# Narrowing float64 weights: a parametric ReLU on ScalarE carries the sign, in place of a VectorE instruction

## The chip, the cores and the metric

The kernel runs on one core of one Trainium2 chip. The metric is the device time of one execution in microseconds (us). Of the kernel before, three runs were timed, and one more execution was taken with the hardware profiler. All timelines below are of that profiled execution, with 0 at the start of its span.

## What is computed

Three blocks follow each other, on 2 batches of 768 positions and a width of 512:

```
# attention: 8 heads of 64; a window of +-15 positions, and 24 block summaries
k_sum = k.reshape(B, H, nb, block, D).max(axis=3)
v_sum = v.reshape(B, H, nb, block, D).mean(axis=3)
a = softmax([scale * q @ k.T in the window, scale * q @ k_sum.T + log(block)])
x = a @ [v, v_sum]
# gated block: 512 -> 1024, a convolution of 3 taps over the positions, 1024 -> 512
h = np.maximum(x @ w_in, 0.0)
conv_out = sum(conv_w[k] * hp[:, k:k + S, :] for k in range(3))
x = h * sigmoid(conv_out) @ w_out
# second block: layer norm, 512 -> 2048 -> 512, and a residual
xn = (x - mu) / np.sqrt(var + 1e-06) * g_ln
out = x + np.maximum(xn @ w_ch1, 0.0) @ w_ch2
```

The activations are float32. The five weights `w_in`, `conv_w`, `w_out`, `w_ch1` and `w_ch2` come as float64, and the kernel turns them into float32 itself.

## The kernel before

**Precision.** Each product of the two dense blocks is made of three matmuls in fp32r: an operand is split into a high part (the value rounded to fp32r) and a low part (what is left), and high*high, high*low and low*high are summed in PSUM. So every weight tile needs a high and a low half before its products can run, and every activation tile too.

**Narrowing.** A float64 weight lies in SBUF as two 32-bit words, the more significant one at the odd place. `weight_ops` (L687) makes of a tile of 128x512 weights its two fp32r halves in six steps, each an operation of its own in the plan:

- z, `narrow_0` (L664), VectorE: the lower word is shifted right by 29, which leaves the three mantissa bits that a float32 still needs from it.
- a, `narrow_1` (L668), VectorE: the sign bit of the upper word is put into bit 31 of the lower word (an AND and an OR in one instruction).
- b, `narrow_2` (L674), ScalarE: the upper word, read as a float32, is multiplied by 2^-112 and its absolute value is taken. Read this way, eight of the eleven exponent bits stand where float32 has its exponent; the factor takes off the difference of the two biases, and the sign goes.
- c, `narrow_3` (L678), VectorE: the upper word is shifted left by three, and the lower word is ORed in: the float32.
- d, ScalarE (L692): the high half. It is followed by e, GpSimd (L694): the low half by a subtraction.

There are 48 such tiles: 8 of `w_in` (names wst and x2a in the profile), 8 of `w_out` (wst), and 32 of the second block (raw; 16 pairs, one of `w_ch1` and one of `w_ch2` for each of 16 slices m of the 2048 columns). The 24x128 tile of `conv_w` (craw) takes the same way in `c1` to `c3` (L894 to L900).

**The work.** Attention goes by 24 windows of 64 positions, four to a group (L497 to L614): scores (sc, L502), their maximum (X, L521), exponentials (prob, L533), the sum's reciprocal (L541, L545), a product (N, L552), a transposition (P, L562), the product with v (av, L582) and its split into the high and low half of xT (L611 gives the low one). The gated block goes by 48 steps i, eight to a group of four windows: three products h (L753), ReLU (L765), three taps on VectorE (c, L781), tanh (L786), gate (g, L794), its split (ghi L805, glo L812), and eight steps later two output tiles x (L825). Step 24 is the first of group 3, the first of the second batch; it needs the low halves of windows 12 to 16. For the second block each batch needs a layer norm: statistics (L1061), normalization (xn, L1120), 32 block transpositions (xf, L1132) and a split (xnT, L1141 gives the low half). Then, in the order of `order` (L1083), for each pair of a batch and a slice m come two halves of ch (L1201, evacuated by L1208 and L1212, two PSUM banks in turn) and six accumulating tiles acc (L1236). The first eight slices of batch 0 come first, then batch 1 with all 16, then the last eight of batch 0.

**What sets the order.** No engine's order is written by hand. Each of these pieces of work is an operation of `Plan` (L26) with an engine, a guessed cost, the operations that it comes after, rings of buffers that it takes and gives back, and a due time. `arrange` (L77) lays them out in one pass: of those that could start soonest it takes the one with the earliest due time, moved by a table of numbers for each kind (`BIAS`, in `KNOBS`, L3). Due times run backwards through the dependencies and subtract the costs (L71 to L75). The kernel then emits all operations by the planned start. So an operation that is taken out also changes the due times and the places of others, on all engines. The numbers of `KNOBS` choose the engine of each operation by its kind and number, so no work goes to another engine.

Each engine runs its instructions in the order given. Loads are issued by SyncE's queue. The raw tiles of the second block have two buffers; the load for slice m waits until e of slice m-2 is done.

Of the kernel before, what the change touches and what calls it, by code (L numbers as in the profile page):

```python
# [13 lines left out]
U32 = mybir.dt.uint32  # L14
BF16 = mybir.dt.bfloat16
AF = mybir.ActivationFunctionType
ALU = mybir.AluOpType
# [2 lines left out]

NEG = -1e9
F64_SCALE = 2.0 ** -112
LN32 = (3.46875, -0.003021240234375, 7.152557373046875e-06)


# [169 lines left out]
def local_summary_attention_moe_kernel(  # L195
# [34 lines left out]
    V, A, G, T = nc.vector, nc.scalar, nc.gpsimd, nc.tensor  # L230
    if O('CAL', '0') == '1':
        import builtins
        V, A, G, T = (builtins.PROXY(x, y) for x, y in ((V, 'V'), (A, 'A'), (G, 'G'), (T, 'P')))
# [51 lines left out]
    plan = Plan()  # L285
# [58 lines left out]
    def make_mask_r(e):  # L344
# [8 lines left out]
        ln = mask_r[64:67, :, 0:NB]  # L353
        G.memset(ln, LN32[0])
        for i in (0, 1):
            G.affine_select(out=ln, in_=ln, compare_op=ALU.is_ge, fill=LN32[i + 1], base=i,
                            pattern=[[0, 3], [0, NB]], channel_multiplier=-1)
# [306 lines left out]
    def narrow_0(raw):  # L664
        least = raw.bitcast(U32)[..., 0::2]
        V.tensor_scalar(out=least, in0=least, scalar1=29, scalar2=None, op0=ALU.logical_shift_right)  # L666

    def narrow_1(raw):  # L668
        w_ = raw.bitcast(U32)
        most, least = w_[..., 1::2], w_[..., 0::2]  # L670
        V.scalar_tensor_tensor(out=least, in0=most, scalar=0x80000000, in1=least,  # L671
                               op0=ALU.bitwise_and, op1=ALU.bitwise_or)

    def narrow_2(raw):  # L674
        f = raw.bitcast(U32)[..., 1::2].bitcast(F32)
        A.activation(out=f, in_=f, func=AF.Abs, scale=F64_SCALE)  # L676

    def narrow_3(raw):  # L678
        w_ = raw.bitcast(U32)
        most, least = w_[..., 1::2], w_[..., 0::2]  # L680
        V.scalar_tensor_tensor(out=most, in0=most, scalar=3, in1=least,  # L681
                               op0=ALU.logical_shift_left, op1=ALU.bitwise_or)

    def narrowed(raw):
        return raw.bitcast(U32)[..., 1::2].bitcast(F32)

    def weight_ops(name, raw, hi, lo, after, extra=()):  # L687
        a = plan.op(name + "z", (("V", 335),), lambda e: narrow_0(raw()), after)
        a = plan.op(name + "a", (("V", 602),), lambda e: narrow_1(raw()), [a])
        b_ = plan.op(name + "b", (("A", 520),), lambda e: narrow_2(raw()), [a])  # L690
        c_ = plan.op(name + "c", (("V", 602),), lambda e: narrow_3(raw()), [b_])
        d = plan.op(name + "d", (("A", 520),), lambda e: A.copy(hi(), narrowed(raw())), [c_] + list(extra))  # L692
        g = plan.op(name + "e", (("G", 1225),),
                    lambda e: G.tensor_tensor(out=lo(), in0=narrowed(raw()), in1=hi().bitcast(F32), op=ALU.subtract),  # L694
                    [d])
        return [d, g]
# [9 lines left out]
    def weight(j, early_reads):  # L706
        t = w_stage(j)

        def ld():
            if j < NF:  # L710
                nc.sync.dma_start(out=t.bitcast(U32).rearrange("p (c f) -> p c f", c=4),
                                  in_=w_in[:, 256 * j:256 * j + 256].rearrange("(c p) f -> p c f", p=128))
            else:
                nc.sync.dma_start(out=t.bitcast(U32), in_=w_out[128 * (j - NF):128 * (j - NF) + 128, :])
        prev = j - 6 if j in (6, 7, 8) else j - 3 if j > 8 else None
        l = dma(f"lw{j}", 1456, ld, WD[prev] if prev is not None else [])
        if j < NF:
            raw = lambda: t.rearrange("p (c f) -> p c f", c=4)
            hl = [lambda i=i: wi[i][:, :, 128 * j:128 * j + 128] for i in range(2)]
        else:  # L720
            raw = lambda: t

            def piece(i):
                if not wo:
                    wo.extend(m1.tile([128, NF, DM], F32R, tag=f"wo{k_}", name=f"wo{k_}") for k_ in range(2))
                return wo[i][:, j - NF, :]
            hl = [lambda i=i: piece(i) for i in range(2)]
        WD[j] = weight_ops(f"w{'io'[j // NF]}{j}", raw, hl[0], hl[1], [l], early_reads if j >= NF else ())
# [7 lines left out]
    def m_step(i):  # L736
# [81 lines left out]
        for t in range(2):  # L818
# [10 lines left out]
            if f == NF - 1:  # L829
                def fe(e, t=t):  # L830
# [8 lines left out]
    craw = at.tile([24, 256], F32, name="craw")  # L839
    lc = [dma("lc0", 70, lambda: nc.sync.dma_start(out=craw.bitcast(U32),  # L840
                                                   in_=conv_w.rearrange("k (f p) -> (k f) p", p=256))),
# [51 lines left out]

    def c1(e):  # L894
        narrow_0(craw)
        narrow_1(craw)

    def c3(e):
        narrow_3(craw)
# [2 lines left out]
    def c4(e):  # L902
        live["cc"] = bank("x2")
        T.transpose(live["cc"][:, 0:28], crow, ident[0:28, 0:28])

    cc = plan.op("cc1", (("V", 464),), c1, lc[:1])
    cc = plan.op("cc2", (("A", 230),), lambda e: narrow_2(craw), [cc])
    cc = plan.op("cc3", (("V", 464),), c3, [cc])
    cc = plan.op("cc4", (("P", 60),), c4, [cc, ident_op, lc[1]], take=[("x2", "cc")])
# [187 lines left out]
    def w2_ops(m, due):  # L1097
        gate = gate2 if m < NS else gate3
        l = dma(f"lwy{m}", 2912, lambda: w2_load(m), gate2, take=[("raw", m)])
        free = [x for t in range(NT) for x in AC[1, m - 8, t]] if m >= 8 else []  # L1100
        for h in range(2):
            s = slice(h * 512, (h + 1) * 512)
            d, g = weight_ops(f"y{m}{h}", lambda h=h: raws[m][:, h * 1024:(h + 1) * 1024],
                              lambda s=s: slots[m % 8][0][:, s], lambda s=s: slots[m % 8][1][:, s], [l], gate + free)
            g.give.append(("raw", m))
            d.due0 = g.due0 = due
            WD2.setdefault(m, []).extend([d, g])
# [245 lines left out]
```

## Time and profile before

| | |
|---|---|
| runs | 548.56, 549.22, 549.1 us; median 549.1 |
| profiled execution | 548.64 us, of which the span is 546.9 and 1.74 lie outside |
| busy share of the span | PE (TensorE) 92%, DVE (VectorE) 70%, ACT (ScalarE) 43%, POOL (GpSimd) 31% |
| instructions | PE 2830, DVE 711, ACT 623, POOL 192 |
| TensorE's granted clock | 0.991 on average |

In the profile an engine is PE, DVE, ACT, POOL or SP, and PEld is TensorE's weight load. A row of a group reads: line, engine, operation, output<-input, shape, count, then busy time in us and the mean of one in ns, then the engine's idle time ahead of it and what ended that. A chain is followed back from the last instruction: at each step to what released it, or to the instruction ahead of it on its engine. Matmuls overlap, so a busy PE is not a PE at its peak.

### The profile page before, as it was taken

The page shows a single profiled execution, that of the slowest core. Times are in us where ns is not written, and L with a number is a line of the kernel's source. Part 1 is how long each engine was busy: PE and PEld are TensorE (multiplying, and loading weights), DVE is VectorE, ACT ScalarE, POOL GpSimd, SP SyncE. Part 2 cuts the span into 40 slices and gives each one's busy share as a digit, 9 for nine tenths or more (in the row PEclk, how much of TensorE's full clock was granted, in tenths as well). Part 3 has the DMA queues.
Part 4 walks back from the last instruction along what each step waited for, and adds up shares of the span by engine and source line. Part 5 has one row for each costly group of instructions (what it writes and reads, how often), then busy time and mean ns, then how long its engine had stood idle before and what let it go on. Part 6 is the DMA issues. An engine that isn't in the chain of part 4 may idle for free.

```text
span 546.9 us, 7840 instructions
## 1 busy us (share of the span) xinstructions
PE 500.9 (92%) x2830; PEld 438.5 (80%) x2830; DVE 383.5 (70%) x711; ACT 233.9 (43%) x623; POOL 169.4 (31%) x192
## 2 busy tenths in 40 slices
PE   7776788798999999889998879999999999999997
PEld 4565767677989898668787768989889899899895
DVE  5799899999988689999999999417767101221104
ACT  5887577643786555554434243123343101101100
POOL 6349457442722342523335410023423000000000
PEclk9999799899999999999999999999999999999999
DMA  9994364234011004000053440024340000020003
GB/s 279 326 237 113 87 182 132 73 76 95 2 32 43 1 13 155 1 1 2 1 188 120 153 141 14 1 77 119 114 155 1 0 1 0 1 115 1 0 1 115
DMA packets 56034, 43.30 MB, mean 79 GB/s; under 512 B 26080, under 2 KB 50940, under 8 KB 55996
## 3 DMA queue, kind: packets, MB, share of 16 engines
q1 hardware_dynamic: 55852, 42.68, 26.3%
q8 instruction: 22, 0.36, 0.3%
q14 instruction: 16, 0.13, 0.1%
q10 hardware_dynamic: 144, 0.13, 0.1%
HBM read 39.22 MB, written 3.15 MB: 77 GB/s over the span
## 4 chain that ended last, share of the span: by engine, by line
PE 49%; DVE 37%; ACT 6%; issue 4%; POOL 2%; DMA 2%; DVEq 0%; SPq 0%; POOLq 0%; ACTq 0%
PE ch L1201 19%; PE acc L1236 19%; DVE c L781 7%; DVE xf L1132 5%; PE x L825 4%; PE h L753 3%; DVE g L794 3%; DVE xT L611 2%; ACT prob L533 2%; DVE raw L671 2%; DVE wst L671 2%; DMA raw<-in_moe_w_ch_dram 2%; DVE raw L681 2%; PE sc L502 1%; DVE wst L666 1%
## 5 line engine op out<-in xcount | busy, mean ns | idle before, releaser
L1236 PE MATMUL acc<-wh,ch 128*128 128x512 f32 x382 | 124.5, 394 | 0.0
L1212 DVE SCALAR_TENSOR_TENSOR ch<-ch,ch 128x384 fp32r<-128x384 f32 x64 | 34.1, 552 | 120.1 <-ACT ch L1208 119.9
L1201 PE MATMUL ch<-xnT,wh 128*128 128x384 f32 x512 | 101.7, 339 | 8.6 <-DVE ch L1212 7.5
L1201 PEld LDWEIGHTS ch<-xnT,wh 128*128 128x128 f32 x512 | 90.3, 188 | 15.1 <-DVE ch L1212 9.9
L753 PE MATMUL h<-xT,wi 128*128 128x258 f32 x576 | 82.8, 294 | 12.4 <-ACT h L765 11.9
L1208 ACT ACTIVATE ch<-ch 128x384 fp32r<-128x384 f32 x64 | 29.5, 490 | 147.0 <-PE acc L1236 140.4
L753 PEld LDWEIGHTS h<-xT,wi 128*128 128x128 f32 x576 | 75.9, 195 | 19.6 <-ACT h L765 17.2
L1236 PEld LDWEIGHTS acc<-wh,ch 128*128 128x128 f32 x382 | 71.7, 188 | 15.7
L694 POOL TENSOR_TENSOR wl<-raw,wh 128x512 fp32r<-128x512 f32 x32 | 47.0, 1488 | 102.7 <-ACT wh L692 61.1
L1236 PE MATMUL acc<-wl,ch 128*128 128x512 f32 x191 | 75.1, 393 | 0.0
L825 PE MATMUL x<-wo,ghi 128*128 128x512 f32 x192 | 62.2, 403 | 0.7 <-ACT x2b L293 0.6
L812 POOL TENSOR_TENSOR glo<-g,ghi 128x256 fp32r<-128x256 f32 x48 | 41.6, 869 | 65.3 <-ACT ghi L805 64.0
L781 DVE SCALAR_TENSOR_TENSOR c<-h,ccol,c 128x256 f32<-128x256 f32 x96 | 56.6, 603 | 3.4 <-ACT c L293 1.6
L1201 PE MATMUL ch<-xnT,wl 128*128 128x384 f32 x256 | 55.0, 336 | 0.0
L1201 PEld LDWEIGHTS ch<-xnT,wl 128*128 128x128 f32 x256 | 45.3, 188 | 0.1
L1236 PEld LDWEIGHTS acc<-wl,ch 128*128 128x128 f32 x191 | 35.8, 188 | 7.1
L825 PE MATMUL x<-wo,glo 128*128 128x512 f32 x96 | 38.0, 396 | 0.4 <-POOL xT L594 0.4
L825 PEld LDWEIGHTS x<-wo,ghi 128*128 128x128 f32 x192 | 33.3, 189 | 6.2 <-ACT x2b L293 1.1
L533 ACT ACTIVATE prob<-sc,nm 128x120 f32<-128x120 f32 x96 | 33.3, 363 | 10.5 <-DVE nm L521 10.4
L1132 DVE STREAM_TRANSPOSE xf<-xn 32x384 f32<-32x384 f32 x64 | 36.4, 569 | 1.4
L786 ACT ACTIVATE c<-c 128x256 f32<-128x256 f32 x48 | 20.0, 419 | 39.8 <-DVE c L781 39.6
L676 ACT ACTIVATE raw<-raw 128x512 f32<-128x512 f32 x32 | 20.6, 682 | 37.2 <-DVE raw L671 20.9
(140 smaller groups left out, 729.5 us busy)
## 6 DMA issues: line engine op xcount, KB each, us to landing
raw<-in_moe_w_ch_dram SPq DMA_DIRECT2D x32, 512.0 KB, 5.4
wst<-in_moe_w_out_dram SPq DMA_DIRECT2D x8, 512.0 KB, 3.5
vw<-in_v_dram SPq DMA_DIRECT2D x20, 192.0 KB, 3.3
wst<-in_moe_w_in_dram SPq DMA_DIRECT2D x5, 512.0 KB, 5.9
s_q<-in_q_dram SPq DMA_DIRECT2D x4, 512.0 KB, 4.8
early<-in_k_dram SPq DMA_DIRECT2D x3, 512.0 KB
early<-in_v_dram SPq DMA_DIRECT2D x3, 512.0 KB, 6.0
x2a<-in_moe_w_in_dram SPq DMA_DIRECT2D x3, 512.0 KB, 8.4
```

What stands on the lines that cost most here:

```text
L533: A.activation(out=pr[:, p, :], in_=sc[:, p * NK:(p + 1) * NK], func=AF.Exp, bias=nm[:, p:p + 1], scale=1.0, accum_out=sm[:, p:p + 1])
L671: V.scalar_tensor_tensor(out=least, in0=most, scalar=0x80000000, in1=least, op0=ALU.bitwise_and, op1=ALU.bitwise_or)
L694: lambda e: G.tensor_tensor(out=lo(), in0=narrowed(raw()), in1=hi().bitcast(F32), op=ALU.subtract),
L753: T.matmul(live["h", i][:, 0:CH + 2], w_[:, c, f * 128:(f + 1) * 128], x_[:, c, :], start=(k_ == 0 and c == 0), stop=(k_ == 2 and c == 3))
L781: V.scalar_tensor_tensor(out=ct, in0=ht[:, kk:kk + CH], scalar=ccol[:, kk * NF + f:kk * NF + f + 1], in1=ct, op0=ALU.mult, op1=ALU.add)
L812: on[e].tensor_tensor(out=glo, in0=live.pop(("g", i)), in1=live["ghi", i].bitcast(F32), op=ALU.subtract)
L825: T.matmul(x2ps[g, t], l[:, ts_], r[:, f, :], start=(f == 0 and j == 0), stop=(f == NF - 1 and j == 2))
L1132: V.transpose(out=o_, in_=i_)
L1201: T.matmul(cp[:, 0:384], w_[:, c * 128:(c + 1) * 128], x_[:, c, s], start=(n_ == 0), stop=(n_ == 11))
L1208: A.activation(out=chs[b, m][0][:, s], in_=live[key][:, 0:384], func=AF.Relu)
L1212: V.scalar_tensor_tensor(out=lo[:, s], in0=live.pop(key)[:, 0:384], scalar=0.0, in1=hi[:, s].bitcast(F32), op0=ALU.max, op1=ALU.subtract)
L1236: T.matmul(acc[key], l[:, ts_], r[:, 512:1024], start=(mm == 0 and j == 0), stop=(done and j == 2))
```

## The change

Step b becomes a parametric ReLU with the same factor 2^-112 and a slope of -2^32 for negative inputs. A positive input gives what it gave. A negative input gives its absolute value times 2^32 more, that is, a 1 in bit 28 of the word, which in positive ones is 0. The shift by three in step c moves that bit to bit 31, the sign. So the sign no longer has to be carried in the lower word, and step a goes, with its 48 instructions on tiles of 128x512 and the one on craw. Step b now comes after the load instead of after a, and c comes after z and b, which write different words and no longer wait for each other.

```diff
+F64_SIGN = -(2.0 ** 32)
...
-    def narrow_1(raw):
-        w_ = raw.bitcast(U32)
-        most, least = w_[..., 1::2], w_[..., 0::2]
-        V.scalar_tensor_tensor(out=least, in0=most, scalar=0x80000000, in1=least,
-                               op0=ALU.bitwise_and, op1=ALU.bitwise_or)
...
-        A.activation(out=f, in_=f, func=AF.Abs, scale=F64_SCALE)
+        A.activation(out=f, in_=f, func=AF.Prelu, scale=F64_SCALE, alpha=F64_SIGN)
...
         a = plan.op(name + "z", (("V", 335),), lambda e: narrow_0(raw()), after)
-        a = plan.op(name + "a", (("V", 602),), lambda e: narrow_1(raw()), [a])
-        b_ = plan.op(name + "b", (("A", 520),), lambda e: narrow_2(raw()), [a])
-        c_ = plan.op(name + "c", (("V", 602),), lambda e: narrow_3(raw()), [b_])
+        b_ = plan.op(name + "b", (("A", 520),), lambda e: narrow_2(raw()), after)
+        c_ = plan.op(name + "c", (("V", 602),), lambda e: narrow_3(raw()), [a, b_])
...
     def c1(e):
         narrow_0(craw)
-        narrow_1(craw)
```

The instructions of PE, ACT, POOL and SP are the same in number and kind before and after; DVE has 49 fewer. Every engine gets a new order, since the plan is laid out anew with the same `KNOBS`. In the changed kernel z is L667, b is L671 and c is L676; lines further down move up by six or seven.

On DVE at the first weight tiles of `w_in`, in the stretch of the first windows, stands before (L666 is z, L671 a, L681 c; L521 to L545 belong to the windows):

```order
L666 TENSOR_SCALAR wst<-wst 128x512
L541 TENSOR_SCALAR sm<-sm 128x4
L671 SCALAR_TENSOR_TENSOR wst<-wst 128x512
L545 RECIPROCAL sm<-sm 128x4
L541 TENSOR_SCALAR sm<-sm 128x4
L666 TENSOR_SCALAR wst<-wst 128x512
L545 RECIPROCAL sm<-sm 128x4
L681 SCALAR_TENSOR_TENSOR wst<-wst 128x512
L671 SCALAR_TENSOR_TENSOR wst<-wst 128x512
```

and now (L667 is z, L676 c):

```order
L667 TENSOR_SCALAR wst<-wst 128x512
L542 TENSOR_SCALAR sm<-sm 128x4
L546 RECIPROCAL sm<-sm 128x4
L542 TENSOR_SCALAR sm<-sm 128x4
L667 TENSOR_SCALAR wst<-wst 128x512
L546 RECIPROCAL sm<-sm 128x4
L676 SCALAR_TENSOR_TENSOR wst<-wst 128x512 x2
L660 COPY vw_91<-vsum 24x1024
```

The two instructions of step a are gone from between, and the two of step c stand together.

On PE, the rows that end with the first product of step 24 (L753 before, L747 now), at the windows of the second batch. Before:

```order
L562 MATMUL tr<-ident,prob 120x128 x4
L496 LDWEIGHTS mask_l
L496 MATMUL sc<-mask_r,mask_l 128x480
L502 MATMUL sc<-kw_87,qb_89 128x120 x4
L562 MATMUL tr<-ident,prob 120x128 x4
L825 MATMUL x_1773<-wo_755,ghi 128x512
L825 MATMUL x_1773<-wo_756,ghi 128x512
L825 MATMUL x_1773<-wo_755,glo 128x512
L825 MATMUL x_1783<-wo_755,ghi 128x512
L825 MATMUL x_1783<-wo_756,ghi 128x512
L825 MATMUL x_1783<-wo_755,glo 128x512
L753 MATMUL h<-xT,wi_81 128x258 x8
```

and now:

```order
L583 MATMUL av<-probT,vw_91 128x128 x4
L819 MATMUL x_1368<-wo_696,ghi 128x512
L819 MATMUL x_1368<-wo_697,ghi 128x512
L819 MATMUL x_1368<-wo_696,glo 128x512
L819 MATMUL x_1328<-wo_696,ghi 128x512
L819 MATMUL x_1328<-wo_697,ghi 128x512
L819 MATMUL x_1328<-wo_696,glo 128x512
L819 MATMUL x_1368<-wo_696,ghi 128x512
L819 MATMUL x_1368<-wo_697,ghi 128x512
L819 MATMUL x_1368<-wo_696,glo 128x512
L747 MATMUL h<-xT,wi_81 128x258 x8
```

Step 24 has moved ahead: counted through the whole order, 40 output tiles x of three matmuls stand ahead of it before and 32 now, 21 windows' scores and masks before and 17 now, 19 transpositions P before and 17 now, and one transposition of q or k fewer. The products with v ahead of it are 17 in both.

On DVE at the slices 2 and 3 of the second block, where the layer norm of batch 1 begins (L1212 and L1205 evacuate ch). Before:

```order
L666 TENSOR_SCALAR raw<-raw 128x512 x2
L671 SCALAR_TENSOR_TENSOR raw<-raw 128x512 x2
L1120 TENSOR_SCALAR xn_3203<-x2b,mv,rs 128x512
L681 SCALAR_TENSOR_TENSOR raw<-raw 128x512 x2
L666 TENSOR_SCALAR raw<-raw 128x512 x2
L671 SCALAR_TENSOR_TENSOR raw<-raw 128x512 x2
L1120 TENSOR_SCALAR xn_3203<-x2b,mv,rs 128x512
L681 SCALAR_TENSOR_TENSOR raw<-raw 128x512 x2
L1120 TENSOR_SCALAR xn_3203<-x2b,mv,rs 128x512
L1132 STREAM_TRANSPOSE xf<-xn_3203 32x3x4x32 x2
L1212 SCALAR_TENSOR_TENSOR ch_3272<-ch,ch_3271 128x384
```

and now:

```order
L1205 SCALAR_TENSOR_TENSOR ch_3232<-ch,ch_3231 128x384 x2
L667 TENSOR_SCALAR raw<-raw 128x512 x2
L676 SCALAR_TENSOR_TENSOR raw<-raw 128x512 x2
L1113 TENSOR_SCALAR xn_3229<-x2b,mv,rs 128x512
L667 TENSOR_SCALAR raw<-raw 128x512 x2
L1125 STREAM_TRANSPOSE xf<-xn_3229 32x3x4x32
L676 SCALAR_TENSOR_TENSOR raw<-raw 128x512 x2
L1125 STREAM_TRANSPOSE xf<-xn_3229 32x3x4x32 x4
L1205 SCALAR_TENSOR_TENSOR ch_3311<-ch,ch_3310 128x384 x2
```

A tile's VectorE work is two rows instead of three, and the evacuations of ch stand in pairs. Counted through the order up to the 15th of these evacuations, DVE has 34 instructions of step a fewer, four of step c and two of step z more, and else the same.

## The prediction

> **What bounds the kernel now.** I read the page's shares and slices first, then the chain that ended last, then a table of three stages cut where the chain changes engine. Busy shares:
>
> ```profile
> PE 500.9 (92%) x2830; PEld 438.5 (80%) x2830; DVE 383.5 (70%) x711; ACT 233.9 (43%) x623; POOL 169.4 (31%) x192
> DVE  5799899999988689999999999417767101221104
> PE 49%; DVE 37%; ACT 6%; issue 4%; POOL 2%; DMA 2%; DVEq 0%; SPq 0%; POOLq 0%; ACTq 0%
> ```
>
> PE looks like the bound, but DVE is full from the second slice to the 25th, and 37% of the chain is its. Two places cut the span: the first product of step 24, and the start of the steady run of the second block, in the chain in order of time:
>
> ```profile
> 168.55 0.85 DVE L611 TENSOR_TENSOR xT<-av,xT 64x256 fp32r<-64x256 f32 x2
> 169.61 1.61 PE L753 MATMUL h<-xT,wi 128*128 128x258 f32 x12
> ...
> 333.22 0.60 DVE raw L671
> 334.33 0.60 ACT xnT L1138
> 335.32 0.61 DVE xnT L1141
> 335.93 0.48 DVE ch L1212
> 336.45 4.51 PE ch L1201 x24
> 340.96 3.50 PE acc L1236 x15
> ```
>
> Step 24 starts when DVE ends the low half of window 16. The steady run starts when DVE, through with the last piece of the layer norm, frees a bank of ch; from there the chain is PE's to the end. The stages:
>
> ```profile
> core 0: us, PE busy (x) PEld busy (x) DVE busy (x) ACT busy (x) POOL busy (x), PEclk, DMA share, GB/s
> 0.00:169.60 169.60, 141.88 (x924) 119.51 (x925) 153.80 (x298) 115.44 (x352) 87.28 (x115) 0.97 0.50 135
> 169.60:336.40 166.80, 152.35 (x872) 132.94 (x870) 154.69 (x295) 79.11 (x194) 59.61 (x61) 1.00 0.20 65
> 336.40:546.90 210.50, 206.66 (x1035) 186.09 (x1035) 75.03 (x120) 39.37 (x79) 22.51 (x16) 1.00 0.13 46
> ```
>
> Stages 1 and 2 are DVE's, with 15.8 and 12.1 us of idle time in 169.6 and 166.8; in stage 2 PE is hardly less busy (152.35). Stage 3 is PE's, and DVE stands idle for two thirds of it. So the change in time is the change of three lengths: when step 24 starts, how long stage 2 takes, and what is left for stage 3.
>
> **What the change removes.** Step a, by its groups, with the spread of its largest:
>
> ```profile
> L671 DVE SCALAR_TENSOR_TENSOR raw<-raw 128x512 uint32<-128x512 uint32 x32 | 27.1, 876 | 0.0
> L671 DVE SCALAR_TENSOR_TENSOR wst<-wst 128x512 uint32<-128x512 uint32 x13 | 10.7, 825 | 0.1
> L671 DVE SCALAR_TENSOR_TENSOR x2a<-x2a 128x512 uint32<-128x512 uint32 x3 | 2.1, 688 | 0.0
> L671 DVE SCALAR_TENSOR_TENSOR craw<-craw 24x128 uint32<-24x128 uint32 x1 | 1.0, 977 | 0.0
> L671 DVE SCALAR_TENSOR_TENSOR raw<-raw x32: 675/686/1803, 221.4 to 413.6; 128x512 uint32<-128x512 uint32 x32
> 307.63 1.20 DVE raw L671 x2
> ```
>
> Most take 0.686, two in a row take 1.20, so one costs the queue 0.60; the means are higher because a few are stretched to 1.8. One of these, at 282.81, ran beside GpSimd's low halves:
>
> ```profile
> 282.81 2.41 DVE L671 SCALAR_TENSOR_TENSOR raw<-raw 128x512 uint32<-128x512 uint32 x2
> 281.03 3.03 POOL L694 TENSOR_TENSOR wl<-raw,wh 128x512 fp32r<-128x512 f32 x2 [2.34 <-ACT wh L692]
> ```
>
> Of 2.41, 1.2 is work; the rest passes while the other engine is at its tile. With a gone, such a wait can fall on the next DVE instruction instead, so I take 0.60 for a tile and keep the mean for the range. The Trainium skill has a rule for this (SBUF — State Buffer, "SBUF: two separate sides"): a VectorE instruction with two inputs in SBUF and a GpSimd instruction exclude each other for their whole length. The trace agrees at 282.81; by that rule step c, which has two inputs as well, would inherit the wait, and the sum stands at 0.60 a tile rather than at the mean.
>
> *Stage 1.* All 16 tiles of the first weights and craw lie in it: 16 x 0.60 + 0.98 = 10.6 us of DVE work gone. The new order also puts behind the low half of window 16 four maxima, two statistics, one evacuation of a probability tile, one of x, and seven instructions of a few numbers:
>
> ```profile
> L521 DVE TENSOR_REDUCE nm<-sc 128x4 f32<-128x480 f32 x24 | 15.5, 651 | 1.9 <-PE sc L502 1.5
> L1061 DVE BATCH_NORM_STATS2 st<-x2a 128x6 f32<-128x512 f32 x6 | 4.1, 679 | 0.0
> L541 DVE TENSOR_SCALAR sm<-sm 128x4 f32<-128x4 f32 x24 | 8.7, 362 | 4.5 <-ACT prob L533 4.3
> ```
>
> The two evacuations taken like a statistic, that is 4 x 0.65 + 4 x 0.68 + 7 x at most 0.36, about 7, less the overlap 6. So step 24 comes 16.6 earlier if DVE's 15.8 us of idle time stay, and less if it now waits more. It will wait more: the work beside it (ACT's exponentials, PE's products) is no shorter. I take 3 of a possible 6 back: -13.6.
>
> *What PE still has to do then.* Ahead of step 24 the new PE order has eight output tiles x, four windows' scores, two P and one transposition less; all of it lands in stage 2.
>
> ```profile
> 168.38 1.39 PE x L825 x6
> 169.77 1.45 PE h L753 x12
> 140.39 0.88 PE sc L502 x8
> 173.57 0.87 PE tr L562 x8
> ```
>
> At 1.39 for two tiles x, 0.88 for a window's scores and 0.87 for two transpositions this is 5.6 + 3.5 + 1.3 = 10.4, and with the four mask products about 11 us.
>
> *Stage 2.* DVE: 17 tiles fewer (-10.2), the 6 us moved in, and by the count of the order four c (0.60 each) and two z (0.37) more: 154.7 - 10.2 + 6 + 3.1 = 153.6. PE: 152.35 + 11, less one acc tile moved behind the start (0.70, a fifth of the 3.50 above) = 162.7. PE becomes the longer of the two. The bounds are 162.7 without any idle time and 177.2 with all of today's 14.5. Some of that idle time is DVE's queue, some is the latency of a step:
>
> ```profile
> PE h L753 <- ACT h L765: 11.9, 10, 2.1
> PE ch L1201 <- DVE ch L1212: 7.5, 5, 2.4
> ACT raw L676 <- DVE raw L671: 20.9, 10, 5.3
> DVE raw L666 <- DMA raw<-in_moe_w_ch_dram: 1.1, 2, 0.8
> ```
>
> The waits for the evacuation of ch should mostly go, since DVE's queue ahead of it is shorter; the waits for the ReLU of h are a round trip. I take 168, that is, 5.3 us idle: +1.4 against 166.8.
>
> *Stage 3.* The order of PE is the same but for that acc tile: +0.7. The last 14 instructions of a lie here and cost nothing now: DVE works 75 us in 210.5. If that cover were gone, they would cost 14 x 0.60.
>
> *The ReLU itself.* No parametric ReLU is in this trace. Its rows' neighbours:
>
> ```profile
> L676 ACT ACTIVATE raw<-raw x32: 654/684/705, 222.1 to 414.4; 128x512 f32<-128x512 f32 x32
> L692 ACT CAST wh<-raw x32: 639/665/689, 223.9 to 418.8; 128x512 fp32r<-128x512 f32 x32
> L293 ACT ACT_TABLE_LOAD x1 | 1.3, 1283 | 0.8 <-PEq L1337 0.8
> ```
>
> A plain cast of the shape takes 0.665, the absolute value 0.684: I take 0.684, no change, since both ends of what ACT does to such a tile lie within 3%; twice that, a second pass, would be 33 us more on ACT over the whole run.
>
> *The waits.* Step b now waits for the load where it waited for a (20.9 us in ten waits). Queued behind it on ACT stand casts and ReLUs of ch, for which DVE and PE wait. DVE's z, which now waits for the same loads, lost 1.1 us to them in two waits, with evacuations of ch behind it, and a still later b is covered by that; uncovered it is at most 0.8 for each of 14 loads. The chain of a tile gets shorter by z and a, which pays where a raw buffer is awaited. On SP the order of the loads changes by a few places in stage 1 and not at all in stage 2; I give it nothing.
>
> **The sum.** -13.6 + 1.4 + 0.7 = -11.5; the profiled execution took 548.64 (0.46 below the median of the runs), so 537.1, forecast 537. Its own range: stage 1 -16.6 to -10.6, stage 2 -4.1 to +6: 529 to 545.
>
> **Rivals.** *DVE sets the whole of stages 1 and 2.* Then the 34 instructions of a ahead of the steady run count in full: 33 x 0.60 + 0.98 = 20.8, less the 3.1 of c and z, plus 0.7: -17.0, 531.6. If the stretched part goes too, the 34 count by their means, 17 x 0.88 + 13 x 0.83 + 3 x 0.69 + 0.98 = 28.8, and the time is 523.6. For it speaks that stage 2 ends in DVE's chain now. Against the lower part speaks PE: with step 24 at 153.0 its 162.7 end at 315.7 even without any idle time, which is 20.7 earlier and gives 528.6, and less needs a step 24 still earlier. I put it at 528.6, with 523.6 to 531.6 as its range; its upper end touches my forecast's lower one.
>
> *Slower: stage 2 becomes PE's with its idle time kept.* A step's round trip (product, ReLU, taps, tanh, gate, split, product) is not shortened by the change, and the 11 us moved behind step 24 come on top. Then stage 2 takes 177.2, +10.4, and the kernel is slower as soon as step 24 gains less than 11.1 us. That happens if windows 12 to 16, which the new order sets closer together with fewer tiles x between them, run by their own latency and DVE's saving turns into waiting. With a gain of 5 there, 554.7; with none, 559.7. For it speak the 11.9 us of waits of h for its ReLU; against it, that DVE is busy in 153.8 of stage 1's 169.6.
>
> *No change*: the two effects cancel within 1.1 us, 549.
>
> *The ReLU is not in the table that ACT has loaded.* Then each change between it and an exponential or tanh costs a load of 1.283. The steps b stand in 13 groups among those in ACT's new order: 26 loads, 33 us on ACT, of which perhaps 20 in DVE's way: 557. The new order has a single table load, at the start, as the trace has, which speaks strongly against it. The Trainium skill states the price of such a switch as about 2.66 us with the drain (ScalarE: Activation LUTs, "What ACT_TABLE_LOAD costs") and in "Table sets: the hidden batching unit" names exp, tanh, relu and abs in one set, the parametric ReLU not among the names; by that price it would be 69 us. The trace has 1.283 for the load and no switch to measure.
>
> **How the numbers follow.** Forecast 0.60, DVE throughout 0.17, no change 0.05, the slower PE stage 0.16, table loads 0.02. A measurement of this kernel tells 0.2%, 1.1 us, from no change. Faster: 0.60 + 0.17 = 0.77; same 0.05; slower 0.18. The range runs from 523, where the DVE case ends, to 553, which takes in the slower case up to a gain of 7 at step 24; left out are most of that case and the table loads, under 0.2.
>
> **What would show it.** Right: step 24's first product near 156 and the steady run near 324 in the changed profile, PE idle some 5 us between them, b at 0.68, one table load, and from there an unchanged 210.5 to 211. Wrong: step 24 later than 163, or stage 2 longer than 172, or waits of c or of ch's ReLU behind b for a load.

## The result, and the profile after

| | before | after |
|---|---|---|
| runs, median | 549.16 us (548.56 to 549.79) | 537.07 us (536.9 to 537.96) |
| profiled span | 546.9 us | 535.2 us |
| first product of step 24 | 169.61 | 148.96 |
| steady run starts | 336.45 | 324.37 |

The changed kernel takes 0.9778 of the time before, with an interval of 0.9764 to 0.9793: 12.1 us less. The forecast was 537.

The shares, the DVE row of the slices and the chain's shares by engine, from the page of the changed kernel:

```profile
PE 500.4 (94%) x2830; PEld 441.4 (82%) x2830; DVE 347.5 (65%) x662; ACT 231.8 (43%) x623; POOL 166.0 (31%) x192
DVE  5689998999769878999979993244554110221104
PE 64%; DVE 23%; issue 5%; ACT 5%; POOL 2%; DMA 1%; DVEq 0%; POOLq 0%; ACTq 0%
```

DVE lost 36 us of busy time and 49 instructions; the chain is PE's for 64% of the span instead of 49%. DVE still stands at 9 in slices 17 to 24, the later half of the second stage, but for a 7 in slice 21. The same two cuts as before, in PE's timeline of the changed kernel (first the 24th step's product, then the steady run's first product of ch):

```profile
148.96 1.61 PE L747 MATMUL h<-xT,wi 128*128 128x258 f32 x12
...
324.37 1.55 PE L1194 MATMUL ch<-xnT,wh 128*128 128x384 f32 x8
```

And the stages between them, as a table of windows:

```profile
0.00:149.00 149.00, 130.38 (x853) 111.65 (x854) 128.19 (x265) 107.29 (x318) 81.04 (x109) 0.97 0.56 151
149.00:324.50 175.50, 163.16 (x942) 143.35 (x941) 157.53 (x299) 87.77 (x231) 62.23 (x67) 0.99 0.20 64
324.50:535.20 210.70, 206.89 (x1039) 186.40 (x1037) 61.83 (x98) 36.70 (x76) 22.74 (x16) 1.00 0.13 46
```

Columns are as before: length, then busy time and count of PE, PEld, DVE, ACT and POOL, the granted clock and the DMA. Stage 1 is 20.65 us shorter (169.61 to 148.96), stage 2 is 8.6 longer (166.84 to 175.41), stage 3 takes 0.4 more (210.45 to 210.83). The removed instructions alone were counted at 10.6 us in stage 1, so about half of what the stage gains comes with the new order, and stage 2 gives part of it back. PE's waits in stage 2, of before and then of after:

```profile
PE ch L1201 <- DVE ch L1212: 6.5, 4, 2.4
PE h L753 <- ACT h L765: 5.0, 4, 1.9
PE x L825 <- ACT x2b L293: 0.6, 1, 0.6
```

```profile
PE x L819 <- ACT ghi L799: 2.9, 2, 2.5
PE ch L1194 <- DVE ch L1205: 2.9, 4, 1.7
PE h L747 <- ACT h L759: 2.6, 2, 1.7
PE x L819 <- ACT x2b L294: 2.4, 2, 1.2
```

The columns are total, times and longest. The waits for ch and for the ReLU of h halve; the output tiles x, eight more of which now lie in this stage, wait for 5.3 us (2.9 and 2.4) where they waited for 0.6. PE is idle for 175.50 - 163.16 = 12.3 us where it was idle for 14.5.

The ReLU itself, and the table, by groups and shapes:

```profile
L671 ACT ACTIVATE raw<-raw 128x512 f32<-128x512 f32 x32 | 20.6, 686 | 5.9 <-DMA raw<-in_moe_w_ch_dram 5.8
L294 ACT ACT_TABLE_LOAD x1 | 1.3, 1283 | 0.8 <-PEq L1330 0.8
```

0.686 us against 0.682 for the absolute value, and one table load in the whole run. Step b waits 5.8 us for loads, in place of 20.9 for step a.

### The profile page after: what moved, and what is told of

The parts are those of the page before. It is cut to its first block, busy times and chain, and to the rows that moved or that the text cites. A ratio compares the mean times of both kernels' runs of the same rounds, so it can differ in the third digit from the quotient of the medians.

```text
span 535.2 us, 7801 instructions
## 1 busy us (share of the span) xinstructions
PE 500.4 (94%) x2830; PEld 441.4 (82%) x2830; DVE 347.5 (65%) x662; ACT 231.8 (43%) x623; POOL 166.0 (31%) x192
## 4 chain that ended last, share of the span: by engine, by line
PE 64%; DVE 23%; issue 5%; ACT 5%; POOL 2%; DMA 1%; DVEq 0%; POOLq 0%; ACTq 0%
PE ch L1194 21%; PE acc L1229 21%; PE h L747 8%; PE x L819 6%; DVE xf L1125 6%; DVE c L775 4%; PE av L583 3%; PE sc L503 2%; DVE xnT L1134 2%; DVE raw L676 1%; ACT prob L534 1%; DVE g L788 1%; ACT qb L294 1%; DVE ch L1205 1%; PE tr L563 1%
## 5 line engine op out<-in xcount | busy, mean ns | idle before, releaser
L1205 DVE SCALAR_TENSOR_TENSOR ch<-ch,ch 128x384 fp32r<-128x384 f32 x64 | 33.7, 551 | 136.1 <-ACT ch L1201 135.8
L747 PE MATMUL h<-xT,wi 128*128 128x258 f32 x576 | 83.0, 294 | 5.4 <-ACT h L759 5.4
L747 PEld LDWEIGHTS h<-xT,wi 128*128 128x128 f32 x576 | 76.6, 196 | 9.2 <-ACT h L759 7.1
L819 PE MATMUL x<-wo,ghi 128*128 128x512 f32 x192 | 63.7, 413 | 5.3 <-ACT ghi L799 2.9
L775 DVE SCALAR_TENSOR_TENSOR c<-h,ccol,c 128x256 f32<-128x256 f32 x96 | 59.2, 619 | 5.2 <-POOL c L298 2.0
L806 POOL TENSOR_TENSOR glo<-g,ghi 128x256 fp32r<-128x256 f32 x48 | 39.1, 816 | 59.7 <-ACT ghi L799 55.2
L583 PE MATMUL av<-probT,vw 120*128 120x128 f32 x192 | 26.9, 284 | 7.6 <-issue 3.4
```

Of the source, the lines that this page charges most:

```text
L583: T.matmul(av[:, p * 128:(p + 1) * 128], vv[:, p], ps[:, p, :], start=True, stop=True)
L747: T.matmul(live["h", i][:, 0:CH + 2], w_[:, c, f * 128:(f + 1) * 128], x_[:, c, :], start=(k_ == 0 and c == 0), stop=(k_ == 2 and c == 3))
L775: V.scalar_tensor_tensor(out=ct, in0=ht[:, kk:kk + CH], scalar=ccol[:, kk * NF + f:kk * NF + f + 1], in1=ct, op0=ALU.mult, op1=ALU.add)
L806: on[e].tensor_tensor(out=glo, in0=live.pop(("g", i)), in1=live["ghi", i].bitcast(F32), op=ALU.subtract)
L819: T.matmul(x2ps[g, t], l[:, ts_], r[:, f, :], start=(f == 0 and j == 0), stop=(f == NF - 1 and j == 2))
L1205: V.scalar_tensor_tensor(out=lo[:, s], in0=live.pop(key)[:, 0:384], scalar=0.0, in1=hi[:, s].bitcast(F32), op0=ALU.max, op1=ALU.subtract)
```

## The experiments

Two theories stood at the start. Theory one: the new order gives back in stage 2 what it gains in stage 1, since it only moves some 11 us of PE's work behind step 24. Theory two: stage 2 keeps its idle time by latency whatever the order, so the saving counts once. Each comparison below is with runs of the kernel before on the same chip (medians of 549.25 to 549.31).

**The saving in the old order.** The plan keeps an operation of a's cost between z and b, and issues nothing for it. So every engine has the order of before, without the instructions of a (the edit is shown against the changed kernel):

```diff
-        b_ = plan.op(name + "b", (("A", 520),), lambda e: narrow_2(raw()), after)
-        c_ = plan.op(name + "c", (("V", 602),), lambda e: narrow_3(raw()), [a, b_])
+        a = plan.op(name + "a", (("V", 602),), lambda e: None, [a])
+        b_ = plan.op(name + "b", (("A", 520),), lambda e: narrow_2(raw()), [a])
+        c_ = plan.op(name + "c", (("V", 602),), lambda e: narrow_3(raw()), [b_])
```

> The order of the kernel before, kept on every engine by leaving step a in the plan with its cost and letting it issue nothing; the parametric ReLU as in the change. Theory one (the new order gives back in stage 2 what it gains in stage 1, since it moves 11 us of PE work behind step 24): here both stages gain, stage 1 about 14 and stage 2 about 5, so about 529 us, 525 to 533, with step 24 near 155 and the steady run near 317. Theory two (stage 2 keeps its idle time by the latency of its steps whatever the order, so the saving counts only once): 537, 535 to 540, like the change.

Measured: 531.09 us, a ratio of 0.9665 (0.9647 to 0.9683), 6.0 less than the change. Its windows:

```profile
0.00:160.14 160.14, 138.96 (x924) 117.62 (x925) 142.81 (x281) 115.18 (x352) 84.04 (x115) 0.99 0.53 143
160.14:319.31 159.17, 151.53 (x872) 133.03 (x870) 144.64 (x276) 78.81 (x195) 56.66 (x61) 1.00 0.21 68
319.31:529.50 210.19, 206.43 (x1035) 186.07 (x1035) 65.27 (x105) 38.49 (x80) 22.61 (x16) 1.00 0.13 46
```

Without a new order the removal shortens both stages, by 9.5 and 7.7 us. So the change is two things: an instruction removed, worth -18.2 (549.28 to 531.09), and an order laid out anew, which costs +6.0. By stages the order makes -11.2, +16.2 and +0.6. Theory two, which expected 537, falls. The total lies where theory one expected it, though not by its parts: stage 1 gains 9.5 instead of about 14, stage 2 gains 7.7 instead of about 5, and the new order gives back more than it gains. One reservation: the granted clock was 0.997 on average here and 0.991 in the profile before, and PE's same instructions took 496.9 us instead of 500.9, so up to 4 of the 18 us may be the clock's.

**The new order with the work still in it.** The order of the change, with a two-input instruction of a's size right behind each z, which changes no value. The planner doesn't know of its time:

```diff
     def narrow_0(raw):
         least = raw.bitcast(U32)[..., 0::2]
         V.tensor_scalar(out=least, in0=least, scalar1=29, scalar2=None, op0=ALU.logical_shift_right)
+        V.scalar_tensor_tensor(out=least, in0=least, scalar=0x80000000, in1=least,
+                               op0=ALU.bitwise_and, op1=ALU.bitwise_or)
```

> The order of the changed kernel with a stand-in for step a on VectorE (two inputs in SBUF, same shape, result unchanged) right behind each z. It shows what the new order costs without the saving. Theory one: slower than the kernel before by what the order gives back, about 8 us, 557, 553 to 561. Theory two: the order is neutral, 549, 547 to 551.

Measured: 573.49 us, ratio 1.0436 (1.0419 to 1.0452), with step 24 at 162.82 and stages of 187.74 and 221.24 behind it. With the work of a in it, the new order is 24 us worse than the old one; without it, 6. Both theories missed this by far (557 and 549). Order and saving don't add up: the removal is worth 18 in the old order and 36 in the new. The granted clock was lower here, 0.93 and 0.95 in the first two stages against 0.97 and 0.99 in the changed kernel, and PE's same instructions took 513.3 us in all instead of 500.4. So a slower PE accounts for at most about 13 of the 36; how much of these it makes was not measured apart.

**The absolute value in the new order.** The changed kernel with `AF.Abs` in step b again, which leaves out the weights' sign:

```diff
-        A.activation(out=f, in_=f, func=AF.Prelu, scale=F64_SCALE, alpha=F64_SIGN)
+        A.activation(out=f, in_=f, func=AF.Abs, scale=F64_SCALE)
```

> The changed kernel with the absolute value in place of the parametric ReLU, so the weights lose their sign (left out here); the instructions are otherwise the same. Both theories: 537, within 0.2%, with step b at 0.68 us; if the parametric ReLU itself costs something, this one is faster by 48 times that.

Measured: 537.45 us (537.06 to 538.23), against 537.07 (536.9 to 537.96) with the parametric ReLU: no difference. Step b took 0.683 here and 0.686 there.

**Half of the saving, in the old order.** Step a is gone for the 16 tiles of the first weights and craw (here), or for the 32 raw tiles (the next one); the other tiles keep a and the absolute value. The edit is that of the first experiment, with a condition on the name; `new` also chooses between the parametric ReLU and the absolute value in `narrow_2`:

```diff
+        new = name[0] == "w"
-        a = plan.op(name + "a", (("V", 602),), lambda e: None, [a])
-        b_ = plan.op(name + "b", (("A", 520),), lambda e: narrow_2(raw()), [a])
+        a = plan.op(name + "a", (("V", 602),), lambda e: None if new else narrow_1(raw()), [a])
+        b_ = plan.op(name + "b", (("A", 520),), lambda e: narrow_2(raw(), new), [a])
```

> The order of the kernel before, with step a gone for the first 16 tiles and craw alone (stage 1); the 32 raw tiles keep it. Theory one: stage 1 gains about 14 and stage 2 is as before, so 535, 532 to 538. Theory two: the earlier step 24 is partly waited away in stage 2, where DVE still has its 17 instructions, so 541 or more.

Measured: 539.5 us, ratio 0.9818 (0.9792 to 0.9843), -9.8. Its windows:

```profile
0.00:159.03 159.03, 136.98 (x925) 115.56 (x926) 142.52 (x281) 115.18 (x352) 84.41 (x115) 0.99 0.55 144
159.03:326.70 167.67, 153.79 (x873) 134.50 (x871) 155.36 (x294) 79.04 (x194) 57.07 (x61) 0.99 0.20 65
326.70:537.10 210.40, 206.65 (x1035) 186.08 (x1035) 74.57 (x120) 39.32 (x79) 22.52 (x16) 1.00 0.13 46
```

Step 24 comes 10.6 us earlier, and stage 2 is only 0.8 longer than before: what stage 1 gains is passed on, not waited away. Theory two falls here too. But theory one's size is missed: a gain of 14, 535 us, was expected, and 539.5 lies outside its 532 to 538. Stage 1 holds the same instructions in the same order here as in the first experiment, and its length differs by 1.1 us (159.03 and 160.14); so much a stage can differ from one execution to another.

**The other half.** `new = name[0] == "y"`, and craw keeps its a.

> The order of before on every engine; step a is gone for the 32 tiles of the channel weights (raw) alone, whose b is the parametric ReLU, and stays for the other 16 tiles and craw, whose b stays the absolute value. The complement of the run with the first 16 tiles, which took 9.8 us off; all of them together took 18.2 off. Theory one (in the old order each instruction of a that leaves DVE's queue ahead of the steady run counts by itself, wherever it stands): the rest, 18.2 - 9.8 = 8.4, so 540.8, step 24 near 169 and stage 2 near 158 to 160. Rival (the late tiles pay only because stage 2 starts earlier, or the two savings share one wait): under 4 us, 545 or more, with stage 2 over 163.

Measured: 539.19 us, ratio 0.9819 (0.9798 to 0.984), -10.1. The first two of its windows:

```profile
0.00:169.46 169.46, 141.68 (x925) 119.46 (x925) 153.48 (x298) 115.22 (x352) 87.66 (x115) 0.97 0.50 135
169.46:327.85 158.39, 151.47 (x872) 133.01 (x870) 143.94 (x276) 78.70 (x195) 56.72 (x61) 1.00 0.20 68
```

Stage 1 stays, stage 2 is 8.5 shorter. The halves give 9.8 and 10.1, together 19.9, where both at once give 18.2: additive within the intervals of the two halves (each over 1 us either way), and each half in its own stage. This one came out as theory one expected, 540.8 with stage 2 at 158 to 160.

**What of the new order costs.** The change tells the planner two things: a's time on VectorE is gone, and b waits for the load alone. The first of two kernels tells it only the second: a's cost stays in the account behind z, and nothing is issued. Both edits are shown against the changed kernel.

```diff
         a = plan.op(name + "z", (("V", 335),), lambda e: narrow_0(raw()), after)
+        a = plan.op(name + "a", (("V", 602),), lambda e: None, [a])
         b_ = plan.op(name + "b", (("A", 520),), lambda e: narrow_2(raw()), after)
```

> The changed kernel's computation; in the planner's account a place of a's cost on VectorE is kept behind z (nothing is issued for it), while b waits for the load alone, as in the change. So of the two things that the change tells the planner, only the new wait of b is told. Theory one (the loss of 6 us against the old order comes from the freed time of a in the account, which lets the planner set scores and probabilities ahead of tiles x): about 531, with stage 2 near 159. Rival (it comes from b's new place): about 537, with stage 2 near 175. Third (the planner's table of numbers fits one order; any order laid out anew loses some us): 534 to 545 here and in the run beside this one.

The second tells it only the first: a's cost is gone, b waits for z and c for b.

```diff
-        b_ = plan.op(name + "b", (("A", 520),), lambda e: narrow_2(raw()), after)
-        c_ = plan.op(name + "c", (("V", 602),), lambda e: narrow_3(raw()), [a, b_])
+        b_ = plan.op(name + "b", (("A", 520),), lambda e: narrow_2(raw()), [a])
+        c_ = plan.op(name + "c", (("V", 602),), lambda e: narrow_3(raw()), [b_])
```

> The counterpart: a is gone from the planner's account as in the change, but b waits for z, as it waited for a before, and c for b. Theory one (the freed time in the account makes the loss): about 537, step 24 near 149 and stage 2 near 175. Rival (b's new wait makes it): about 531, step 24 near 160 and stage 2 near 159. Third (any order laid out anew with this table loses): 534 to 545.

Measured: 532.45 us (ratio 0.97, 0.9678 to 0.9721) with the cost kept, 538.72 (0.9803, 0.9778 to 0.9829) with the cost gone; the profiled execution of the latter was its shortest, 536.58. The first two stages, with the cost kept:

```profile
0.00:157.84 157.84, 139.46 (x914) 118.83 (x915) 133.80 (x277) 112.70 (x339) 81.27 (x114) 0.97 0.55 145
157.84:320.87 163.03, 153.97 (x887) 136.77 (x885) 149.59 (x282) 82.18 (x208) 58.24 (x63) 0.99 0.20 66
```

and with the cost gone:

```profile
0.00:153.71 153.71, 131.37 (x886) 110.75 (x887) 134.03 (x271) 109.65 (x323) 79.91 (x112) 0.99 0.58 149
153.71:325.45 171.74, 160.45 (x917) 140.28 (x916) 152.16 (x293) 84.26 (x225) 58.27 (x64) 0.99 0.19 63
```

The loss comes with the freed time in the account: only the kernel whose planner knows that a is gone puts 160 us of PE's work into stage 2 and comes out near the change. The clock doesn't make this difference: it was 0.986 in the profiled execution with the cost kept, which loses little, and 0.994 with the cost gone, which loses. The step's new wait is worth +1.4 against the first experiment and -1.7 against this last one, whose own runs lie 2.4 apart (536.58 to 539.01). With the cost gone, step 24 was expected near 149 and stage 2 near 175; they came at 153.71 and 171.74. Of the third theory (any new order loses) this much stands: the order laid out with the cost kept is 1.4 behind the old one.

**A stretched instruction of 24 rows.** In the kernel before, step c of craw (24x128) takes 3.85 us, and PE waits 5.7 for what follows from it; in the first experiment 3.85 and 4.3; in the changed kernel 0.27 and 0.7. The tile's rows in the first experiment and in the changed kernel:

```profile
L682 DVE SCALAR_TENSOR_TENSOR craw<-craw x1: 3853/3853/3853, 48.5 to 48.5; 24x128 uint32<-24x128 uint32 x1
  PE x L904: 4.3, 1
```

```profile
L676 DVE SCALAR_TENSOR_TENSOR craw<-craw x1: 273/273/273, 51.6 to 51.6; 24x128 uint32<-24x128 uint32 x1
  PE x L897: 0.7, 1
```

In the first experiment GpSimd was working on tiles one right behind the other; its timeline:

```profile
48.70 0.98 POOL L553 TENSOR_TENSOR prob<-prob,sm 128x480 f32<-128x480 f32 x1
49.64 1.29 POOL L695 TENSOR_TENSOR wi<-x2a,wi 128x512 fp32r<-128x512 f32 x1
50.90 1.29 POOL L695 TENSOR_TENSOR wi<-wst,wi 128x512 fp32r<-128x512 f32 x1
```

Two kernels go at this, both made from the first experiment's. The first takes the second input away:

```diff
-        narrow_3(craw)
+        most = craw.bitcast(U32)[..., 1::2]
+        V.tensor_scalar(out=most, in0=most, scalar1=3, scalar2=None, op0=ALU.logical_shift_left)
```

> The first experiment's kernel (order of before, a gone everywhere: 531.09) with one small instruction changed: step c of craw, the 24x128 one that takes 3.85 us there and 0.27 in the changed kernel, shifts its one input and leaves out the OR with the other (so the low three bits of those 24 rows are left out). In the old order it stands beside GpSimd's low halves. Theory one (it is held up because it has two inputs while GpSimd works on two inputs at the same time): it takes under 0.5 us, the wait of PE for crow, 4.3, falls to about 1, and of the 3.6 us step 24 gets 2 to 3.5 earlier: total 528 to 530. Rival (any instruction of DVE at that place is held, or the long time is a wait for something else, such as its input): it still takes over 3 us and the total stays at 531.

Measured: 530.87 us (ratio 0.9663, 0.9641 to 0.9685), the same as the first experiment, and the row says why:

```profile
L900 DVE TENSOR_SCALAR craw<-craw x1: 3782/3782/3782, 48.4 to 48.4; 24x128 uint32<-24x128 uint32 x1
```

With one input it is held just as long. The theory of the two inputs falls. The second kernel takes GpSimd's tiles away from beside it, by giving two of them to VectorE, where they stand behind craw:

```diff
-                    lambda e: G.tensor_tensor(out=lo(), in0=narrowed(raw()), in1=hi().bitcast(F32), op=ALU.subtract),
+                    lambda e: (V if name in ("wi5", "wi6") else G).tensor_tensor(
+                        out=lo(), in0=narrowed(raw()), in1=hi().bitcast(F32), op=ALU.subtract),
```

> The first experiment's kernel (order of before, a gone everywhere: 531.09, step 24 at 160.14) with the low halves of the sixth and seventh first-weight tile on VectorE instead of GpSimd. In the first experiment GpSimd starts these two at 49.64 and 50.90, right behind a probability tile that ends near 49.7, and the 24x128 step c of craw lasts from 48.5 to 52.4, as long as that stretch; the run with one input showed that its second input is not the cause. On VectorE the two stand behind craw's copy. Theory one (a small VectorE instruction that comes while GpSimd has one two-input tile right behind another is held until GpSimd pauses): c now ends near 49.7, that is 0.3 to 1.3 us long; the wait of PE for crow falls from 4.3 to 1 to 2; two tiles of 0.6 to 0.7 are added to VectorE, so step 24 is 1 to 2.5 earlier and the total 528.5 to 530. Rival (the place in the queue or the instruction itself costs it): c still takes 3.8 and the total is 531 to 532.5.

Measured: 528.76 us, ratio 0.9621 (0.9591 to 0.9651), the lowest median of all, with an interval that still touches the first experiment's (0.9647 to 0.9683). DVE's rows around it:

```profile
47.60 0.69 DVE L682 SCALAR_TENSOR_TENSOR x2a<-x2a 128x512 uint32<-128x512 uint32 x1
...
49.08 1.35 DVE L682 SCALAR_TENSOR_TENSOR craw<-craw 24x128 uint32<-24x128 uint32 x1
50.47 0.48 DVE L901 COPY crow<-craw 24x128 f32<-24x128 f32 x1
...
52.23 0.69 DVE L695 TENSOR_TENSOR wi<-x2a,wi 128x512 fp32r<-128x512 f32 x1
```

and GpSimd's in the same stretch, up to its pause:

```profile
45.44 3.17 POOL L1003 TENSOR_TENSOR s_k<-s_k 96x512 f32<-96x512 f32 x3
48.69 0.65 POOL L1003 TENSOR_TENSOR parts<-s_k 96x64 f32<-96x64 f32 x1
49.31 0.98 POOL L553 TENSOR_TENSOR prob<-prob,sm 128x480 f32<-128x480 f32 x1
50.35 0.52 POOL L638 MEMSET vw<- 24x512 f32 x1
```

The instruction now ends at 50.43, 0.14 after GpSimd's tile (50.29). It ended 0.14 after GpSimd's last tile in the first experiment too (52.33 and 52.19), and 0.08 after it with one input (52.21 and 52.13). The copy behind it meets GpSimd's memset and is held in the same way: it takes 0.48 us and ends 0.08 after the memset, where it takes 0.21 with no GpSimd instruction beside it (the kernel with the cost kept). PE's wait for crow falls from 4.3 to 0.8 and step 24 comes at 158.07 instead of 160.14. The place in the queue is not the cause of the 3.85 us, since it is the same here; GpSimd's unbroken run is. The 2.1 us at step 24 are not the held instruction's alone, as GpSimd also has two tiles less to do and VectorE two more.

## Why the prediction came out right

The total was right and its mechanism in part: a gain in stage 1, a smaller loss in stage 2, and next to nothing in stage 3. But two terms were mis-sized by 7 us each, in opposite directions, and that they cancel to 0.1 us in the total is luck. Of the signs named ahead, the start of the steady run near 324, step b at 0.68, the single table load and the last stage of 210.5 to 211 were met; step 24 near 156 and some 5 us of idle PE in stage 2 were not.

*The removed instructions.* The prediction took 10.6 us in stage 1 and 10.2 of DVE's work in stage 2. In the old order the halves gave 10.6 at step 24 and 8.5 in stage 2, and both together 9.5 and 7.7. DVE's busy time fell by 11.0 and 11.3 in stage 1 and by 10.1 and 10.8 in stage 2 (the first experiment and the halves). That bears out 0.60 a tile for the work: by the means of 0.69 to 0.88 it would have been 13.8 and 14.9. In stage 2 the time fell by less than the work, 7.7 to 8.5.

*Stage 1, "-13.6".* It was -20.65. The term that was mis-sized is the order's: 6 us of moved DVE work less 3 given back, so -3, where the change against the old order without a shows -11.2 (160.14 to 148.96). DVE is busy for 128.19 us there against 142.81, 14.6 less. Of this 3.6 us is the small step c of craw that is no longer held, which the prediction did not look at, though its row was in the trace before. The 16 instructions fewer that DVE has in the stage (265 against 281) come to 7.2 us by the means of their groups in the first experiment, near the 7 that were added up. The rest, some 4 us, is a balance of instructions that both orders have, and that last shorter or longer in the new one. The largest are the first weights' shifts z, 3.4 us less (first experiment, then the changed kernel), and their steps c, 2.6 more (9.7 and 12.3):

```profile
L667 DVE TENSOR_SCALAR wst<-wst 128x512 uint32<-128x512 uint32 x13 | 9.3, 724 | 0.0
L667 DVE TENSOR_SCALAR wst<-wst 128x512 uint32<-128x512 uint32 x13 | 5.9, 452 | 0.1
```

Against the kernel before, DVE's busy time fell by 25.6 where 16.6 was forecast, and its idle time rose by 5.0 (15.8 to 20.8) where 3 was allowed for: the work was mis-sized by 9, the waiting by 2.

*Stage 2, "+1.4".* It was +8.6. (The 168 that the prediction took is 1.2 above 166.8, not 1.4.) PE's work was forecast at 162.7 us and came to 163.16; DVE's was forecast at 153.6 and came to 157.53. "PE becomes the longer of the two" holds for the totals; that it therefore sets the stage, with an idle time of 5.3, is what failed: PE kept 12.3. The chain of waits of the changed kernel shows why, by its first pieces on DVE and the last ones:

```profile
198.13 0.90 PE sc L503 x8
199.06 0.66 DVE nm L522
...
314.69 0.57 DVE xf L1125
315.30 0.57 DVE ch L1205
315.91 4.43 PE ch L1194 x24
```

From 149 to 199 it is PE's alone; from 199 to 316 it is mostly DVE's, but for a stretch of PE's from 261 to 276, with the transpositions of the layer norm (xf) at its end. The windows with these cuts:

```profile
149.00:199.00 50.00, 49.68 (x357) 45.83 (x356) 40.57 (x89) 29.29 (x103) 16.38 (x23) 1.00 0.06 13
199.00:316.00 117.00, 104.98 (x545) 89.84 (x543) 110.42 (x198) 56.16 (x125) 45.86 (x44) 0.99 0.27 91
```

PE is full for 50 us while DVE waits for 9.4 of them; then DVE is busy for 110.42 of 117, and PE waits for 12.0. The stage has two bounds, one behind the other, and neither engine's total sets it. The prediction called DVE full from the second slice to the 25th and compared totals; the slices before already have a 6 for DVE in the 14th (178 to 191 us, early in stage 2), so its load was uneven there too. The new order moved 11.6 us of PE's work (151.53 to 163.16) and 12.9 of DVE's (144.64 to 157.53; 3.4 of it left stage 3) into the stage. By the total of one engine at most 12.9 would have been added to the old order's 159.17; it was 16.2.

*Stage 3, "+0.7"* was +0.4, and the 14 instructions of a in it cost nothing, as said.

*The ReLU at no cost* is confirmed twice, by its row and by the kernel with the absolute value. *The waits of b*: 5.8 us for loads, against "at most 0.8 for each of 14"; the longest was 1.9, so this bound was too low for a single wait. The steps c behind them on the raw tiles waited for nothing (0.0 us of idle time in their row), and the kernels with and without the free b differ by 1.4 and -1.7; a cost of these waits was not seen.

*The rivals.* That DVE sets the whole of stages 1 and 2 (528.6) was wrong for the change, yet it is about what the removal does in the old order (531.09). In the slower rival, stage 2 with its idle time kept (177.2) was nearly right (175.41), and only the part on step 24, a gain under 11.1, was wrong: it was 20.65. The sign of being wrong "stage 2 longer than 172" came (175.41), so by the prediction's own statement its second stage was wrong. The table loads did not come.

What stays open: which of the planner's choices turns the freed time into the longer stage 2, why some instructions last longer in one order than in the other, and how much of the 18 us in the old order (up to 4) and of the 36 between the stand-in and the change (up to about 13) is the clock's.

## What to carry to other kernels

Where a planner lays the program out anew, an edit is two changes, a saving and another order: run the saving in the old order too (keep its place in the plan and issue nothing), since here the order took back 6 of 18 us and the old order with the saving was the better kernel. Read a stage in two or three windows before its bound is named from the totals: two engines that are each full in another part of it set the sum of the parts, not the longer total.

## What the hardware showed that was not expected

A VectorE instruction on 24x128 elements, 0.27 us long elsewhere, was held for up to 3.85 us until GpSimd paused behind a run of three tiles, with two inputs or with one. The Trainium skill (SBUF — State Buffer, "SBUF: two separate sides") has the two engines exclude each other for the length of one instruction, when VectorE's has two inputs in SBUF and GpSimd's reads SBUF, or when VectorE's uses both of its ports in a fast mode. The trace agrees that the instruction is held, and shows it held past the end of the first tile: with starts at 48.70, 49.64 and 50.90 on GpSimd, it ended at 52.33.

Another VectorE instruction with two inputs, a little ahead of it, was not held: c on 128x512 took its 0.69 at 47.60 in the last experiment, beside GpSimd's sums on 96x512 and narrower (45.44 to 48.61). The traces show one difference. In the run of three, each GpSimd tile starts 0.04 us before the one ahead has ended (the first ends at 49.68, the second starts at 49.64), and the pause behind them is 0.06 us. The c at 47.60 started in a gap between two sums, from 47.55 to 47.62, and the sum behind the gap then took 0.99 us, against 0.45 in the changed kernel. So it looks as if an instruction like these gets in only where GpSimd leaves a gap; no run changed the gap by itself.
